# Folding the sequence transform of a Fourier mixing kernel once more for even k: sums and differences of rows s and S/4 - s

## The chip, the cores and the metric

One core of one Trainium2 chip. The metric is the device time of one execution in microseconds, median over runs; executions of one kernel agree within about 0.2% here.

## The reference, cut to what matters

```python
X = np.fft.fft(x, axis=1)            # x: (8, 3008, 256), batch, sequence S, features D
X = np.fft.fft(X, axis=2).real       # only the real part goes on
h = X.reshape(24064, 256) @ w_in     # w_in: (256, 2048)
g = np.maximum(0.01 * h, h)
out = g @ w_out                      # w_out: (2048, 256)
```

## The kernel before

The two products with w_in and w_out take most of the time ("up", line 422, and "down", lines 465 and 485). The feature transform is folded into w_in at the start. The sequence transform remains as matmuls with tables of cosines and sines (lines 350 and 354, tile `dft_ps`). Symmetries shrink it: x is loaded as four mirrored parts that are added and subtracted on VectorE (DVE), output frequencies k are treated by parity c, rows s by parity r. A "unit" is one batch and one parity of k; it has two feature halves (`blk`), so a batch has four transforms.

```python
NI = 3                       # chunks of 128 rows per parity of s: six in all
KW, KF = [377, 376], [189, 188]
...
def fold_rows(t, h):         # mirrored rows and features
    a, z = t[:, h, 0], t[:, h, 1]
    nc.vector.tensor_tensor(a, a, z, op=ALU.add)
    ...
def fold_halves(b, t):       # rows s and S/2 - s
    a, z = t[:, :, 0], t[:, :, 1]
    nc.vector.tensor_tensor(a[:, 0], z[:, 0], z[:, 1], op=ALU.add)
    nc.vector.tensor_tensor(a[:, 1], z[:, 0], z[:, 1], op=ALU.subtract)
    zs[b] = a
...
def sequence(z_of, m, part, c):
    pe, po = dft_ps(), dft_ps()
    kf, kw = KF[c], KW[c]
    tab = tabs[2 * part, c]
    for i, (lo, hi) in enumerate(((0, kf), (kf, 2 * kf), (0, 2 * kf))):     # even s
        nc.tensor.matmul(pe[0:m, lo:hi], lhsT=z_of(i, 0), rhs=tab[:, i * kf : i * kf + hi - lo], ...)
    tab = tabs[2 * part + 1, c].rearrange("p (i k) -> p i k", i=NI)
    for i in range(NI):                                                     # odd s
        nc.tensor.matmul(po[0:m, 0:kw], lhsT=z_of(i, 1), rhs=tab[:, i, 0:kw], ...)
    return pe, po
...
units = [(b, c) for b in range(B) for c in range(2)]                        # even k first
```

One more input, the Nyquist feature of all eight batches, goes through the same transform with 8 stationary columns instead of 128, once per parity. A scheduler decides the order of each engine's queue from the program order, so source order and engine order can differ.

## Time and profile before

| | before |
|---|---|
| median (3 runs) | 1948.77 us (1948.72 to 1948.90) |
| profiled span | 1947.3 us |
| PE busy | 1924.5 us, 99% |
| DVE busy | 1109.9 us, 57% |
| GpSimd (POOL) busy | 1039.1 us, 53% |

The prediction below shows the lines that carry this. In a timeline each line is: start in us, length in us, engine, source line, operation, output and inputs, stationary operand (partitions * columns), moving operand (partitions x columns), how many instructions were merged, and in brackets the idle time before them with what ended it. Each matmul here, of 32-bit data, is recorded twice, each time with a weight load (six records and six loads for the three matmuls at 697.66 us); I call one such pair of load and matmul a record.

### The profile page before, as it was taken

The numbers are of one execution on the slowest core, as the hardware profiler recorded it, in microseconds if no ns is written. First come the engines' busy times: TensorE is split into PE (matmuls) and PEld (weight loads), VectorE is DVE, ScalarE is ACT, GpSimd is POOL, SyncE is SP. The second block draws the span as 40 slices with busy tenths as digits, with TensorE's granted clock in tenths as the row PEclk, the third lists the DMA queues.
The fourth block names the chain that finished last, engine by engine and source line by source line (L and its number), as shares of the span: only waits on it lengthen the run. The fifth ranks groups of instructions, "written<-read, shape, count | busy, mean of one in ns | idle before, by whom it ended". The sixth has DMA issues, their size and how long they took to land.

```text
span 1947.3 us, 24383 instructions
## 1 busy us (share of the span) xinstructions
PE 1924.5 (99%) x8920; PEld 1683.9 (86%) x8920; DVE 1109.9 (57%) x2143; ACT 458.9 (24%) x526; POOL 1039.1 (53%) x1508
## 2 busy tenths in 40 slices
PE   6999999999999999999999999999999999999999
PEld 3788888888888888888888888888888888888888
DVE  8765545575555655466555665547545574555554
ACT  4422222222222222222222222222222222222221
POOL 1115555565555655556555665556645565555554
PEclk9999999999999999999999999999999999999999
DMA  8120000010001000020000200002000020000000
GB/s 300 42 85 20 11 19 22 19 76 11 19 22 76 19 11 30 11 80 15 22 19 12 83 22 12 19 12 83 22 11 19 11 95 12 19 11 22 11 11 22
DMA packets 25598, 70.22 MB, mean 36 GB/s; under 512 B 4596, under 2 KB 17268, under 8 KB 23432
## 3 DMA queue, kind: packets, MB, share of 16 engines
q1 hardware_dynamic: 23360, 68.66, 9.6%
q8 instruction: 71, 1.16, 0.2%
q14 instruction: 47, 0.39, 0.1%
q10 hardware_dynamic: 2120, 0.02, 0.1%
HBM read 43.95 MB, written 24.71 MB: 35 GB/s over the span
## 4 chain that ended last, share of the span: by engine, by line
PE 98%; DVE 1%; DMA 0%; ACT 0%; issue 0%; SPq 0%; DVEq 0%; ACTq 0%
PE sum_ps L485 56%; PE cos_ps L422 17%; PE sin_ps L422 17%; PE dft_ps L354 3%; PE sum_ps L465 3%; PE dft_ps L350 2%; PE up_ps L312 1%; DMA raw<-in_w_in_dram 0%; DVE power L288 0%; DVE wo L289 0%; ACT L433 0%; DVE e L496 0%; DVE wo L287 0%; ACT g L433 0%; SPq L260 0%
## 5 line engine op out<-in xcount | busy, mean ns | idle before, releaser
L427 DVE SCALAR_TENSOR_TENSOR cos<-nb,wn,cos_ps 128x251 f32<-128x251 f32 (+1 forms) x768 | 330.7, 472 | 721.2 <-PE cos_ps L422 721.1
L433 ACT ACTIVATE g<-g 128x1004 f32<-128x1004 f32 (+1 forms) x384 | 399.1, 1039 | 1208.3 <-DVE g L432 1199.9
L440 POOL TENSOR_TENSOR s<-g 128x251 f32<-128x251 f32 (+1 forms) x368 | 271.8, 739 | 761.1 <-ACT g L433 761.1
L485 PE MATMUL sum_ps<-s,wt 128*128 128x251 f32 (+1 forms) x2208 | 527.7, 374 | 0.0
L485 PEld LDWEIGHTS sum_ps<-s,wt 128*128 128x128 f32 x2208 | 415.9, 188 | 52.4
L422 PE MATMUL cos_ps<-mix,wf 128*128 128x251 f32 (+1 forms) x1536 | 387.9, 375 | 0.0
L422 PE MATMUL sin_ps<-mix,wf 128*128 128x251 f32 (+1 forms) x1536 | 387.6, 374 | 0.0
L485 PE MATMUL sum_ps<-g,wo 128*128 128x251 f32 (+1 forms) x1472 | 371.9, 374 | 0.0
L422 PEld LDWEIGHTS cos_ps<-mix,wf 128*128 128x128 f32 x1536 | 291.2, 190 | 35.8 <-issue 1.6
L422 PEld LDWEIGHTS sin_ps<-mix,wf 128*128 128x128 f32 x1536 | 290.3, 189 | 35.2 <-PE up_ps L312 0.2
L485 PEld LDWEIGHTS sum_ps<-g,wo 128*128 128x128 f32 x1472 | 279.4, 190 | 38.7
L431 DVE TENSOR_TENSOR g<-cos,sin_ps 128x502 f32<-128x502 f32 (+1 forms) x384 | 260.1, 677 | 50.0 <-DVE cos L427 8.9
L441 POOL TENSOR_TENSOR s<-s,g 128x251 f32<-128x251 f32 (+1 forms) x368 | 278.8, 758 | 0.0
L443 POOL TENSOR_TENSOR s<-g,s 128x251 f32<-128x251 f32 (+1 forms) x368 | 262.6, 714 | 28.6
L432 DVE TENSOR_TENSOR g<-cos,sin_ps 128x502 f32<-128x502 f32 (+1 forms) x384 | 257.3, 670 | 0.0
L442 POOL TENSOR_TENSOR s<-g 128x251 f32<-128x251 f32 (+1 forms) x368 | 243.2, 661 | 0.0
L485 PE MATMUL sum_ps<-g,wt 128*128 128x251 f32 (+1 forms) x736 | 215.8, 375 | 0.0
L485 PE MATMUL sum_ps<-s,wo 128*128 128x251 f32 (+1 forms) x736 | 215.7, 375 | 0.0
L485 PEld LDWEIGHTS sum_ps<-s,wo 128*128 128x128 f32 x736 | 139.4, 189 | 16.4
L485 PEld LDWEIGHTS sum_ps<-g,wt 128*128 128x128 f32 x736 | 139.8, 190 | 15.8
L496 DVE TENSOR_TENSOR o<-e,sum_ps 128x251 f32<-128x251 f32 (+1 forms) x184 | 67.5, 409 | 8.7 <-ACT e L494 8.7
L354 PE MATMUL dft_ps<-tab,xt 128*128 128x377 f32 (+1 forms) x192 | 66.0, 479 | 0.0
(53 smaller groups left out, 598.1 us busy)
## 6 DMA issues: line engine op xcount, KB each, us to landing
xt<-in_x_dram SPq DMA_DIRECT2D x16, 1536.0 KB, 10.0
out_dram<-o SPq DMA_DIRECT2D x80, 251.0 KB, 2.3
raw<-in_w_in_dram SPq DMA_DIRECT2D x8, 512.0 KB, 5.4
raw<-in_w_out_dram SPq DMA_DIRECT2D x8, 512.0 KB, 3.9
out_dram<-o SPq DMA_DIRECT2D x16, 250.0 KB, 2.3
nb<-nyq_dram SPq DMA_DIRECT2D x8, 376.5 KB, 4.8
nb<-nyq_dram SPq DMA_DIRECT2D x8, 376.0 KB, 3.2
tab<-in_seq_tab_dram SPq DMA_DIRECT2D x4, 565.5 KB, 10.7
```

What stands on the lines that cost most here:

```text
L354: nc.tensor.matmul(po[0:m, 0:kw], lhsT=z_of(i, 1), rhs=tab[:, i, 0:kw], start=(i == 0), stop=(i == NI - 1))
L422: nc.tensor.matmul(pt[blk][:, h * n : (h + 1) * n], lhsT=wf[:, blk, fs], rhs=mixed[b, c][blk][:, at : at + n], start=True, stop=True)
L427: nc.vector.scalar_tensor_tensor(cos[:, hs], in0=spreads[b, c][:, at : at + n], scalar=wn[:, h * NH + f : h * NH + f + 1], in1=pt[0][:, hs ...
L431: nc.vector.tensor_tensor(g[:, 0], cos[:, 0 : 2 * n], pt[1][:, 0 : 2 * n], op=ALU.add)
L432: nc.vector.tensor_tensor(g[:, 1], cos[:, 0 : 2 * n], pt[1][:, 0 : 2 * n], op=ALU.subtract)
L433: nc.scalar.activation(g, g, ACT.Lrelu)
L440: nc.gpsimd.tensor_tensor(s1, a[1][0], a[1][1], op=ALU.add)
L441: nc.gpsimd.tensor_tensor(s2, s1, a[0][0], op=ALU.subtract)
L442: nc.gpsimd.tensor_tensor(s3, a[0][0], a[1][0], op=ALU.subtract)
L443: nc.gpsimd.tensor_tensor(s4, a[0][1], s2, op=ALU.subtract)
L485: nc.tensor.matmul(sums[j][p], lhsT=still[p], rhs=moving[p], start=(f == 0 and i % 2 == 0), stop=(f == NH - 1), skip_group_check=True)
L496: nc.vector.tensor_tensor(to, x, y, op=ALU.add)
```

## The change

For even k the table of row S/4 - s equals that of row s up to a sign that alternates with k/2. So the two rows can be added for half of the frequencies and subtracted for the other half, and each matmul needs half the columns. The outputs go to every second column. To let the rows meet on the same partition, x is laid out in seven chunks instead of six (four of 95 rows for even s, three for odd s), and DVE makes the sums and differences ("quarter folds"). Odd k, which needs no quarter folds, now comes first in each batch. Core of the diff:

```diff
-NI = 3
+NI = [4, 3]
+NT = 7
+PE_ROWS = 95
+PO_ROWS = 60
+PARITIES = (1, 0)
...
+    def fold_quarters(src, sums, last, tmp):
+        for op, to in zip((ALU.add, ALU.subtract), sums):
+            nc.vector.tensor_tensor(to[0:PE_ROWS, 0:2], src[0:PE_ROWS, 0:2], src[0:PE_ROWS, 2:4], op=op)
+            nc.vector.tensor_tensor(to[:, 4], src[:, 4], src[:, 5], op=op)
+        lo, hi = slice(0, PO_ROWS), slice(P // 2, P // 2 + PO_ROWS)
+        nc.scalar.copy(tmp[0][lo], src[hi, 6])
+        nc.scalar.copy(tmp[1][hi], src[lo, 6])
+        nc.vector.tensor_tensor(last[lo], src[lo, 6], tmp[0][lo], op=ALU.add)
+        nc.vector.tensor_tensor(last[hi], tmp[1][hi], src[hi, 6], op=ALU.subtract)
...
-        for i, (lo, hi) in enumerate(((0, kf), (kf, 2 * kf), (0, 2 * kf))):
+        for i in range(n):                                       # even s: n = 4
+            if c == 1:
+                still, to = rows[0:PE_ROWS, i], pe[0:m, i % 2 * kf : (i % 2 + 1) * kf]
+            else:
+                q, p = divmod(i, 2)
+                still, to = rows[0][(p + part) % 2][0:PE_ROWS, q], pe[0:m, q * kf + p : (q + 1) * kf : 2]
...
-        for i in range(NI):
-            nc.tensor.matmul(po[0:m, 0:kw], lhsT=z_of(i, 1), rhs=tab[:, i, 0:kw], start=(i == 0), stop=(i == NI - 1))
+        for i in range(n):                                       # odd s: n = 3
+            if c == 1:
+                still, to = rows[:, NI[0] + i], po[0:m, 0:kw]
+            elif i < 2:
+                still, to = rows[0][(i + part) % 2][:, NI[0]], po[0:m, i:kw:2]
+            else:
+                still, to = rows[1], po[0:m, 0:kw]
...
-    units = [(b, c) for b in range(B) for c in range(2)]
+    units = [(b, c) for b in range(B) for c in PARITIES]
...
+            if n > 0 and n % 2 == 0 and part > 0 and f == 1:
+                fold_x_quarters(b, part - 1)
```

More of the change, by code (lines that the diff above doesn't have):

```diff
@@ L62 @@
 KP = [1, 0]
-TW = [4 * KF[0], NI * KC]
+TW = [[4 * PE_ROWS, 2 * KW[0]], [4 * KF[1], 3 * KW[1]]]
+PARITIES = (1, 0)
 UW = [753, 752]
@@ L78, in m_order @@
     at = np.arange(P)[:, None]
-    if r == 1:
-        m = at + P * np.arange(NI)
-        return np.where(m < 376, m, -1)
+    if r == 0:
+        m = np.concatenate([2 * at, 2 * at + 1, 376 - 2 * at, 375 - 2 * at], axis=1)
+        last = np.array([188, 187, 190, 189])
+        return np.where(at < PE_ROWS - (last != 188), m, -1)
     half = at // (P // 2)
-    m = np.concatenate([2 * at, 2 * at + 1, 2 * (P + at - half * (P // 2)) + half], axis=1)
-    return np.where(m < 377, m, -1)
+    m = P + at % (P // 2)
+    m = np.where(at % (P // 2) < PO_ROWS, np.where(half, 375 - m, m), -1)
+    return np.concatenate([at, 375 - at, m], axis=1)
 def k_order(c):
@@ L93, in laid_out @@
 def laid_out(x):
-    m = np.stack([m_order(0), m_order(1)], axis=-1)
-    rows = 2 * m + np.arange(2)
+    m = np.concatenate([m_order(0), m_order(1)], axis=1)
+    rows = 2 * m + np.repeat([0, 1], NI)
     d = np.concatenate([np.arange(P + 1), np.arange(D - 1, P, -1)])
@@ L111, in seq_tables, with values @@
 def seq_tables():
-    out = np.zeros((4, 2, P, TW[1]), np.float32)
-    for r in range(2):
-        m = m_order(r)
-        s = 2 * m + r
-        weight = np.where(m < 0, 0.0, np.where((s == 0) | (s == Q), 0.5, 1.0))
-        for c in range(2):
-            k = k_order(c)
-            turn = (s[:, :, None] * k) % S
-            turn = np.where(turn > H, turn - S, turn)
-            a = 2.0 * np.pi * turn / S
-            cos = weight[:, :, None] * np.where(4 * np.abs(turn) == S, 0.0, np.cos(a))
-            sin = weight[:, :, None] * np.where(np.abs(turn) == H, 0.0, np.sin(a))
-            for n, t in ((r, cos), (2 + r, sin)):
-                if r == 1:
-                    out[n, c].reshape(P, NI, KC)[:, :, : KW[c]] = t
-                    continue
-                kf = KF[c]
-                t = t[:, :, :kf]
-                parts = [t[:, 0], t[:, 1], t[:, 2] * (m[:, 2:] % 2 == 0), t[:, 2] * (m[:, 2:] % 2 == 1)]
-                out[n, c, :, : 4 * kf] = np.concatenate(parts, axis=1)
+    out = np.zeros((4, 2, P, TW[1][1]), np.float32)
+    def values(m, r, c):
+        s, k = 2 * m + r, k_order(c)
+        weight = np.where(m < 0, 0.0, np.where((s == 0) | (s == Q), 0.5, 1.0))[:, :, None]
+        turn = (s[:, :, None] * k) % S
+        turn = np.where(turn > H, turn - S, turn)
+        a = 2.0 * np.pi * turn / S
+        cos = np.where(4 * np.abs(turn) == S, 0.0, np.cos(a))
+        sin = np.where(np.abs(turn) == H, 0.0, np.sin(a))
+        return weight * cos, weight * sin
+    for r in range(2):
+        for part, t in enumerate(values(m_order(r), r, 1)):
+            if r == 0:
+                t = t[:, :, : KF[1]]
+            out[2 * part + r, 1, :, : TW[1][r]] = t.reshape(P, -1)
+    for part, t in enumerate(values(m_order(0), 0, 0)):
+        for q in range(2):
+            for p in range(2):
+                v = t[:, q, p : KF[0] : 2]
+                at = (2 * q + p) * PE_ROWS
+                out[2 * part, 0, :, at : at + v.shape[1]] = v
+    m = m_order(1)
+    m[P // 2 :, 2] = m[: P // 2, 2]
+    difference = np.arange(P)[:, None] // (P // 2)
+    for part, t in enumerate(values(m, 1, 0)):
+        last = t[:, 2] * ((np.arange(KW[0]) + part) % 2 == difference)
+        out[2 * part + 1, 0, :, : TW[0][1]] = np.concatenate([t[:, 0, 0::2], t[:, 0, 1::2], last], axis=1)
     return out
@@ L155, in chunks @@
     for b in range(B):
-        for c in range(2):
+        for c in PARITIES:
             for j in range(0, UW[c], CW):
@@ L203, in load_x @@
     def load_x(b, q=None):
-        t = xp.tile([P, 2, 2, NI * 2, D], F32, tag="x", bufs=1, name="xt")
+        t = xp.tile([P, 2, 2, NT, D], F32, tag="x", bufs=1, name="xt")
         for h in range(2):
-            (q or nc.sync).dma_start(t[:, h], x[b, :, h].rearrange("p e i r d -> p e (i r) d"))
+            (q or nc.sync).dma_start(t[:, h], x[b, :, h])
         return t
@@ L226, in fold_halves, with fold_x_quarters @@
         nc.vector.tensor_tensor(a[:, 1], z[:, 0], z[:, 1], op=ALU.subtract)
-        zs[b] = a
+        zs[b] = t
+    def fold_quarters(src, sums, last, tmp):
[7 more added lines that the diff above has]
+        nc.vector.tensor_tensor(last[hi], tmp[1][hi], src[hi, 6], op=ALU.subtract)
+    def fold_x_quarters(b, part):
+        src, z = zs[b][:, part, 0, :, part * P : (part + 1) * P], zs[b][:, part, 1]
+        halves = [z[:, :, i * P : (i + 1) * P] for i in range(2)]
+        fold_quarters(src, halves, halves[0][:, 5], [h[:, 6] for h in halves])
+        quarters[b, part] = halves, halves[0][:, 5]
+    quarters = {}
     feat_sb = const.tile([P, 2, 2 * P], F32, name="feat_sb")
@@ L234, in tile_fnet_leaky_relu @@
     wt = const.tile([P, 4, NH, P], F32, name="wt")
-    nyx = const.tile([P, 2, 2, NI, 2, B], F32, name="nyx")
+    nyx = const.tile([P, 2, 2, NT, B], F32, name="nyx")
     inf = const.tile([P, 2], F32, name="inf")
@@ L240, in load_tab @@
     def load_tab(q, n, c):
-        t = const.tile([P, TW[n % 2]], F32, name=f"tab_{n}_{c}")
-        q.dma_start(t, seq_tab[n, c, :, 0 : TW[n % 2]])
+        t = const.tile([P, TW[c][n % 2]], F32, name=f"tab_{n}_{c}")
+        q.dma_start(t, seq_tab[n, c, :, 0 : TW[c][n % 2]])
         tabs[n, c] = t
@@ L340, in combine_w_out, with sequence @@
             nc.gpsimd.tensor_tensor(to, x, y, op=ALU.subtract)
-    def sequence(z_of, m, part, c):
+    def sequence(rows, m, part, c):
         pe, po = dft_ps(), dft_ps()
         kf, kw = KF[c], KW[c]
-        tab = tabs[2 * part, c]
-        for i, (lo, hi) in enumerate(((0, kf), (kf, 2 * kf), (0, 2 * kf))):
-            nc.tensor.matmul(pe[0:m, lo:hi], lhsT=z_of(i, 0), rhs=tab[:, i * kf : i * kf + hi - lo],
-                             start=(i == 0), stop=(i == NI - 1), skip_group_check=True)
-        tab = tabs[2 * part + 1, c].rearrange("p (i k) -> p i k", i=NI)
-        for i in range(NI):
-            nc.tensor.matmul(po[0:m, 0:kw], lhsT=z_of(i, 1), rhs=tab[:, i, 0:kw], start=(i == 0), stop=(i == NI - 1))
+        tab, n = tabs[2 * part, c], NI[0]
+        for i in range(n):
[4 more added lines that the diff above has]
+                still, to = rows[0][(p + part) % 2][0:PE_ROWS, q], pe[0:m, q * kf + p : (q + 1) * kf : 2]
+            at = i * TW[c][0] // n
+            nc.tensor.matmul(to, lhsT=still, rhs=tab[0:PE_ROWS, at : at + to.shape[1]],
+                             start=(i == 0), stop=(i == n - 1), skip_group_check=True)
+        tab, n, at = tabs[2 * part + 1, c], NI[1], 0
+        for i in range(n):
[5 more added lines that the diff above has]
+                still, to = rows[1], po[0:m, 0:kw]
+            nc.tensor.matmul(to, lhsT=still, rhs=tab[:, at : at + to.shape[1]],
+                             start=(i == 0), stop=(i == n - 1), skip_group_check=True)
+            at += to.shape[1]
         return pe, po
@@ L373, in dft @@
         b, c = u
-        z = zs[b]
-        sums = sequence(lambda i, r: z[:, (c + blk) % 2, 2 * i + r, blk * P : (blk + 1) * P], P, blk, c)
+        if c == 1:
+            rows = zs[b][:, 1 - blk, 0, :, blk * P : (blk + 1) * P]
+        else:
+            rows = quarters.pop((b, blk))
+        sums = sequence(rows, P, blk, c)
         def rest():
@@ L392, in nyquist @@
     def nyquist(c):
-        sums = sequence(lambda i, r: nya[:, c, i, r, :], B, 0, c)
+        if c == 1:
+            rows = nya[:, 1]
+        else:
+            halves = [nyb[:, 0], nyb[:, 1]]
+            fold_quarters(nya[:, 0], halves, halves[0][:, 5], [h[:, 6] for h in halves])
+            rows = halves, halves[0][:, 5]
+        sums = sequence(rows, B, 0, c)
         def rest():
@@ L510, in step @@
                 if part == 0:
-                    if c == 1:
+                    if n % 2 == 1:
                         t = xs.pop(b + 1)
@@ L517, in step @@
                     dft(units[n + 1], part - 1)()
-            if c == 0 and part == 2 and f == 6 and b + 1 < B:
+            if n % 2 == 0 and part == 2 and f == 6 and b + 1 < B:
                 xs[b + 1] = load_x(b + 1)
@@ L532, in tile_fnet_leaky_relu @@
     for n in range(4):
-        load_tab(nc.sync, n, 0)
+        load_tab(nc.sync, n, 1)
     convert(w0)
@@ L542, in tile_fnet_leaky_relu @@
     fold_halves(0, t0)
-    nyquist(0)()
+    nyquist(1)()
     dft(units[0], 0)()
@@ L568, in tile_fnet_leaky_relu @@
     for n in range(4):
-        load_tab(nc.sync, n, 1)
+        load_tab(nc.sync, n, 0)
     convert(o)
+    for blk in range(2):
+        fold_x_quarters(0, blk)
     some_steps(plain)
-    nyquist(1)()
+    nyquist(0)()
     spread(units[1])
@@ L590 @@
         "x": x,
-        "x_nyq": x[..., P].transpose(1, 2, 3, 4, 5, 0),
+        "x_nyq": x[..., P].transpose(1, 2, 3, 4, 0),
         "w_in": moe_w_in,
```

## The prediction

> **What bounds the kernel now.** I read the page first: the busy shares, the slices, the chain that ended last.
>
> ```profile
> PE 1924.5 (99%) x8920; PEld 1683.9 (86%) x8920; DVE 1109.9 (57%) x2143; ACT 458.9 (24%) x526; POOL 1039.1 (53%) x1508
> ...
> PE 98%; DVE 1%; DMA 0%; ACT 0%; issue 0%; SPq 0%; DVEq 0%; ACTq 0%
> PE sum_ps L485 56%; PE cos_ps L422 17%; PE sin_ps L422 17%; PE dft_ps L354 3%; PE sum_ps L465 3%; PE dft_ps L350 2%; PE up_ps L312 1%; DMA raw<-in_w_in_dram 0%; DVE power L288 0%; DVE wo L289 0%; ACT L433 0%; DVE e L496 0%; DVE wo L287 0%; ACT g L433 0%; SPq L260 0%
> ```
>
> The reader is to see that the matmul engine is the bound, and that the change touches a small part of it: the two dft_ps lines are 3% + 2% of the span, about 105 us. A busy PE is not yet a saturated one, so I asked for busy time by stretch (columns: length, then busy time and instruction count of each engine, granted clock, DMA share, GB/s).
>
> ```profile
> 0.00:50.00 50.00, 31.66 (x89) 17.50 (x90) 43.11 (x82) 21.62 (x34) 4.91 (x10) 0.93 0.82 293
> 50.00:140.00 90.00, 90.00 (x407) 75.12 (x406) 64.86 (x116) 29.14 (x39) 14.39 (x21) 1.00 0.18 60
> 140.00:500.00 360.00, 360.00 (x1685) 318.12 (x1685) 198.14 (x387) 82.99 (x92) 202.99 (x297) 1.00 0.08 28
> ...
> 1000.00:1500.00 500.00, 500.00 (x2339) 441.28 (x2338) 283.86 (x547) 113.66 (x127) 285.88 (x412) 1.00 0.08 30
> ```
>
> After 50 us PE has no idle time, at full clock. So every array cycle removed there is time removed, as long as nothing else starts to hold PE up. The first 50 us are different: PE works 32 of them, DVE 43. Next the timeline of one transform of 128 features at about 698 us:
>
> ```profile
> 697.66 1.44 PE L350 MATMUL dft_ps<-tab,xt 128*128 128x189 f32 x6
> 698.94 2.07 PE L354 MATMUL dft_ps<-tab,xt 128*128 128x377 f32 x6
> 700.85 0.37 PE L485 MATMUL sum_ps<-g,wo 128*128 128x251 f32 x1
> ```
>
> Starts count, not durations, because matmuls overlap. Each matmul is recorded twice (six records for three matmuls). The even part, four records of 189 columns and two of 378, takes 698.94 - 697.66 = 1.28 us for 1512 columns; the odd part, six of 377, takes 1.91 us for 2262. Both are 0.845 ns per column and record: here the moving columns alone set the time. One such transform costs 3.19 us.
>
> [...]a load of 128 columns lasts 189 ns and one of 8 columns (the Nyquist rows) 90 ns, so 120 columns cost about 99 ns, with some 83 ns fixed. [...]the 189-column records start every 160 ns though each needs a load recorded at 189 ns.[...]
>
> **The change part by part.** (1) Even k, even s: three matmuls (189 + 189 + 378 = 756 columns) become four of 95, 94, 95, 94 (378 columns). By columns that is 2 x 378 x 0.845 = 0.64 us. But eight records now each need a new 128-column weight load, and a load starts only when the previous matmul starts.[...] (2) Even k, odd s: 3 x 377 = 1131 columns become 189 + 188 + 377 = 754: 2 x 754 x 0.845 = 1.27 us instead of 1.91. These are long enough for their loads (160 ns is seen). One even-k transform thus goes from 3.19 to 2.15 us, 1.04 saved; there are 8 batches x 2 feature halves, 16 x 1.04 = 16.6 us. The one Nyquist transform of even k has 8-column loads, so its short records aren't bound by them: 3.19 to 1.91, 1.3 us more. (3) Odd k: 4 x 188 and 3 x 376 columns, as many as before; 17 transforms with one more matmul each, 0.1 us. PE therefore gives up 16.6 + 1.3 - 0.1 = 17.8 us.
>
> (4) DVE and DMA get more: x has seven chunks instead of six, so loads and folds grow by 1/6. The folds were 28.5 + 19.4 + 18.2 + 16.0 + 14.0 = 96 us, so +16 us; the new quarter folds are 16 x (two of 95x256, two of 128x128, two of 60x128), at rates of existing SBUF operations some 0.35 + 0.35 + 0.2 x 4 = 1.5 us, +24 us. DVE goes to about 1150 us of 1930, 60%: hidden on average, and the question is the burst after each x load. (5) The start: odd k comes first, and its first transform needs the difference of the halves, which DVE makes after the sum.
>
> The start, worked along DVE's queue: before, DVE folds x from 16.34 us and the first x transform starts at 25.48, when the half sum is ready. After: row folds 2 x (2.1 + 1.0 + 1.0), small Nyquist folds 0.7, Nyquist butterfly 0.3, both half folds 2 x 1.95 = 13.1 us, so 29.4 us, 4 us later. PE then idles over 5 us before it, long enough to lose the clock, perhaps 2.5 us more. Against that stands the wait that follows:
>
> ```profile
> 34.55 1.01 PE L422 MATMUL sin_ps<-mix,wf 128*128 128x251 f32 x4
> 41.35 3.72 PE L465 MATMUL sum_ps<-g,wo 128*128 128x251 f32 x8 [5.79 <-ACT g L433]
> 44.86 1.86 PE L312 MATMUL up_ps<-win,feat_sb 128*128 128x512 f32 x2
> ```
>
> Here PE waits 5.8 us, and then runs cold (eight records of 251 columns need 3.5 us instead of 1.7). The order of the changed program puts fifteen down matmuls ahead of the next weight fold, so this wait and the cold stretch shrink. Walking both queues with the durations above I lose 1.3 us by the end of that weight fold and about 1 us in the next: +2.5 us, range 0 to 5. Sum: 1948.8 - 17.8 + 2.5 = 1933.5 us.
>
> **Rivals.** First, **the DVE burst becomes a wait of PE**. In the trace before, around the fold at 1340 us (the longest wait for x):
>
> ```profile
> 1339.91 2.19 DVE L215 TENSOR_TENSOR xt<-xt 128x1536 f32<-128x1536 f32 x1 [1.36 <-DMA xt<-in_x_dram]
> ...
> 1355.16 2.09 DVE L226 TENSOR_TENSOR xt<-xt 128x1536 f32<-128x1536 f32 x1
> 1357.17 0.67 DVE L431 TENSOR_TENSOR g<-cos,sin_ps 128x502 f32<-128x502 f32 x1
> 1357.76 0.67 DVE L432 TENSOR_TENSOR g<-cos,sin_ps 128x502 f32<-128x502 f32 x1
> 1358.35 0.85 DVE L427 SCALAR_TENSOR_TENSOR cos<-nb,wn,cos_ps 128x251 f32<-128x251 f32 x2
> ```
>
> The second g of that step normally frees a PSUM pair 6.0 us before PE needs it; here it came 5.9 us late, a margin of 0.12 us. In the other five bursts like it the margins are 1.3 to 1.9 us. With folds a sixth longer, and x landing later (first half 6.3 us after issue; about 4.2 of it transfer, so +0.7), the same order would stall PE. But the changed program's order puts one fold operation between every cos pair and every g pair, where the old one often put two. Walking it from a first fold at 3.2 us after a cos start, with PE's step of 4.66 us: g pairs come late by 1.9, 2.5, 2.6, 4.2, then 1.8 us, and the quarter folds fall behind that. 4.2 is under 6.0, so no stall; with the longest x wait, 5.3. If I am wrong by 2 us in each of seven bursts, the time is 1945. Second, **the weight loads bind harder**: if the whole 190 ns must pass per short record, the even part takes 1.52 us instead of 1.28, an even-k transform saves only 0.4 us, and the time is about 1944. The 160 ns pitch speaks against it. Third, **the loads bind not at all** (82 ns a record): 0.22 us more per transform, 1930. Fourth, a price of stride-2 PSUM writes: nothing speaks for it; doubled time for those records would cost about 1.3 us a transform, and eat the gain.
>
> **Range and chances.** The gain can't exceed about 21.5 us (16 x 1.26 + 1.3), 1.1% of the time, so faster by over 2% (39 us) is out of reach; slower by over 2% would need several new waits at once. Predicted 1933.5 us, range 1928 (loads hidden, or a free start) to 1943 (loads or bursts costing about 9 us): same 0.98, others 0.01 each.
>
> **What would show it.** In the timeline of an even-k transform: start to start of the eight 95- and 94-column records 0.88 us (0.64: loads hidden; 1.5: whole loads count), then 1.27 us for the odd part. PE still without idle time after 60 us, at clock 1.00, and PE's first sum_ps at about 43 to 45 us instead of 41.35. DVE near 1150 us, with no PE wait on DVE's g or on POOL in the bursts. The prediction is wrong if stride-2 writes or weight loads stretch those records, if PE waits a few us after each x load, or if the start loses more than 5 us.

The forecast's sum came to 1948.8 - 17.8 + 2.5 = 1933.5 us. One term of the 17.8 was built on a load time that was taken from no trace: a short record at 110 ns, so 8 x 0.110 = 0.88 us for the even part, which with 1.27 us for the odd part makes the 2.15 us of an even-k transform and the 1.04 us saved. An estimate from the trace before comes close: loads of 128 and of 8 columns last 189 and 90 ns, 99 ns for 120 columns, so 106 ns for 128; and in the transform at 697.66 us each load starts 1 to 2 ns after a matmul starts. Together that is about 108 ns a record, if nothing but that part of the load has to fit, which was an assumption. The clock that a gap costs is seen in the same trace: after the 5.79 us of waiting before 41.35 us the mean granted clock was 0.50 until 44.86 us; after the 1.84 us before 25.48 us it was 1.00 until 28.74 us. That the new gap would cost 2.5 us was a guess. The 4.2 us of transfer for half of x is near the trace: its two halves, 3.15 MB, moved in some 8.7 us (1333.4 to 1342.1 us), 4.3 us each.

## The result, and the profile after

| | before | after |
|---|---|---|
| median | 1948.84 us (6 runs) | 1936.82 us (6 runs, 1935.49 to 1937.37) |
| profiled span | 1947.3 us | 1935.4 us |
| PE busy | 1924.5 us | 1909.9 us |
| DVE busy | 1109.9 us | 1149.3 us |
| mean granted clock | 0.998 | 0.996 |

The ratio of after to before is 0.9937, 95% interval 0.9924 to 0.9949; a ratio is the mean time of one kernel's runs over that of the other's of the same rounds, so not quite the ratio of the medians. The change won 12.0 us where 15.3 were forecast.

The page after, busy shares and chain:

```profile
PE 1909.9 (99%) x8988; PEld 1687.9 (87%) x8988; DVE 1149.3 (59%) x2245; ACT 468.6 (24%) x560; POOL 1055.4 (55%) x1508
...
PE 98%; DMA 1%; DVE 0%; issue 0%; ACT 0%; SPq 0%; ACTq 0%; DVEq 0%
```

PE is still the bound. The same stretches as before (columns as in the prediction: length, busy time and count of PE, weight loads, DVE, ScalarE (ACT) and GpSimd, clock, DMA share, GB/s):

```profile
0.00:50.00 50.00, 28.86 (x81) 17.28 (x82) 39.26 (x75) 18.97 (x33) 3.25 (x10) 0.87 0.73 267
50.00:140.00 90.00, 90.00 (x418) 76.06 (x417) 76.50 (x145) 32.86 (x49) 12.22 (x18) 1.00 0.21 75
140.00:500.00 360.00, 360.00 (x1706) 320.57 (x1705) 207.09 (x408) 85.23 (x98) 208.75 (x300) 1.00 0.08 30
```

After 50 us PE has no idle time, as before. In the first 50 us it works 28.9 us instead of 31.7, at a mean granted clock of 0.87 instead of 0.93. One even-k transform after, to hold against the one at 698 us before:

```profile
579.22 1.03 PE L402 MATMUL dft_ps<-tab,xt 95*128 95x95 f32 x8
580.08 1.47 PE L412 MATMUL dft_ps<-tab,xt 128*128 128x189 f32 x6
581.39 0.37 PE L554 MATMUL sum_ps<-g,wo 128*128 128x251 f32 x1
```

From start to start the eight short records take 0.86 us and the odd part 1.31, together 2.17 instead of 3.19 us. Single records show why it is not 0.64 for the short ones: their weight loads start at 579.223, 579.333, 579.444, 579.556 us, one every 110 to 112 ns, and the matmuls follow at that pace. The Nyquist transform is a control in the same trace. It has the same 95 rows, the same columns and the same stride-2 outputs, but 8 stationary columns:

```profile
83.07 0.83 PE L402 MATMUL dft_ps<-tab,nyx 95*8 95x95 f32 x8
83.73 1.44 PE L412 MATMUL dft_ps<-tab,nyx 128*8 128x189 f32 x6
```

Its eight records take 0.66 us, 83 ns each: that is near the pace of the columns alone (80 ns at 0.845 ns each). The last view after is PE at the start, to hold against the lines from 34.55 us in the prediction:

```profile
22.09 2.06 PE L412 MATMUL dft_ps<-tab,nyx 128*8 128x376 f32 x6
31.48 2.85 PE L402 MATMUL dft_ps<-tab,xt 95*128 95x188 f32 x8 [7.33 <-issue]
34.12 3.54 PE L412 MATMUL dft_ps<-tab,xt 128*128 128x376 f32 x6
37.50 1.44 PE L402 MATMUL dft_ps<-tab,xt 95*128 95x188 f32 x8
...
47.15 8.33 PE L534 MATMUL sum_ps<-g,wo 128*128 128x251 f32 x30 [2.86 <-ACT g L502]
```

The first x transform starts at 31.48 us (before: 25.48) and takes 37.50 - 31.48 = 6.02 us, the second (same shape) 3.17: after the gap of 7.33 us PE ran at about half clock, and again after the second wait, of 2.86 us. The granted clock, 0.53 in both, stands third from the right:

```profile
31.48:37.50 6.02, 6.02 (x15) 4.52 (x15) 3.63 (x10) 4.19 (x9) 0.00 (x0) 0.53 0.53 154
47.15:50.75 3.60, 3.60 (x9) 2.94 (x10) 3.60 (x10) 2.80 (x5) 0.00 (x0) 0.53 0.13 49
```

The first down matmul starts at 47.15 us (before: 41.35), after a shorter wait, 2.86 instead of 5.79 us.

To put one number on the start, I added up PE's lost time up to 100 us: the time to its first matmul, plus for every record its start-to-start time beyond what a record of that width takes in the steady stretch (short records are priced by their columns, 80 ns). Before: 24.6 us. After: 29.9 us. So the start lost 5.2 us in these two traces; with short records priced at the 110 ns that they take it is 5.0, and the trace of an unedited repeat gives 4.6 to 4.8.

### The profile page after: what moved, and what is told of

Same layout as the page of the kernel before. It is cut to its first block, busy times and chain, and to the rows that moved or that the text cites. A ratio compares the mean times of both kernels' runs of the same rounds, so it can differ in the third digit from the quotient of the medians.

```text
span 1935.4 us, 24654 instructions
## 1 busy us (share of the span) xinstructions
PE 1909.9 (99%) x8988; PEld 1687.9 (87%) x8988; DVE 1149.3 (59%) x2245; ACT 468.6 (24%) x560; POOL 1055.4 (55%) x1508
## 3 DMA queue, kind: packets, MB, share of 16 engines
q1 hardware_dynamic: 23360, 72.09, 10.1%
## 4 chain that ended last, share of the span: by engine, by line
PE 98%; DMA 1%; DVE 0%; issue 0%; ACT 0%; SPq 0%; ACTq 0%; DVEq 0%
PE sum_ps L554 56%; PE cos_ps L491 17%; PE sin_ps L491 17%; PE sum_ps L534 3%; PE dft_ps L412 3%; PE dft_ps L402 2%; PE up_ps L357 1%; DMA raw<-in_w_in_dram 0%; DMA wn_dram<-wf 0%; DVE power L333 0%; DVE e L565 0%; DVE cos L496 0%; ACT g L502 0%; ACTq L369 0%; SPq L305 0%
## 5 line engine op out<-in xcount | busy, mean ns | idle before, releaser
L509 POOL TENSOR_TENSOR s<-g 128x251 f32<-128x251 f32 (+1 forms) x368 | 265.5, 721 | 727.1 <-ACT g L502 722.6
L512 POOL TENSOR_TENSOR s<-g,s 128x251 f32<-128x251 f32 (+1 forms) x368 | 273.0, 742 | 28.9
L500 DVE TENSOR_TENSOR g<-cos,sin_ps 128x502 f32<-128x502 f32 (+1 forms) x384 | 259.5, 676 | 47.9 <-DVE cos L496 11.3
L510 POOL TENSOR_TENSOR s<-s,g 128x251 f32<-128x251 f32 (+1 forms) x368 | 271.4, 738 | 0.0
L511 POOL TENSOR_TENSOR s<-g 128x251 f32<-128x251 f32 (+1 forms) x368 | 263.6, 716 | 0.0
L501 DVE TENSOR_TENSOR g<-cos,sin_ps 128x502 f32<-128x502 f32 (+1 forms) x384 | 257.2, 670 | 0.0
L534 PE MATMUL sum_ps<-g,wo 128*128 128x251 f32 x256 | 58.8, 383 | 2.9 <-ACT g L502 2.9
```

The costliest lines, as they stand in the source:

```text
L500: nc.vector.tensor_tensor(g[:, 0], cos[:, 0 : 2 * n], pt[1][:, 0 : 2 * n], op=ALU.add)
L501: nc.vector.tensor_tensor(g[:, 1], cos[:, 0 : 2 * n], pt[1][:, 0 : 2 * n], op=ALU.subtract)
L509: nc.gpsimd.tensor_tensor(s1, a[1][0], a[1][1], op=ALU.add)
L510: nc.gpsimd.tensor_tensor(s2, s1, a[0][0], op=ALU.subtract)
L511: nc.gpsimd.tensor_tensor(s3, a[0][0], a[1][0], op=ALU.subtract)
L512: nc.gpsimd.tensor_tensor(s4, a[0][1], s2, op=ALU.subtract)
```

## The experiments

Medians are of four to six runs each; "before" stood at 1948.3 to 1948.85 us beside them. An unedited run of the changed kernel in the last group of runs gave 1936.83 us (1935.97 to 1937.27), so differences below 0.7 us are not read.

> The changed kernel itself, unedited, on the chip and in the rounds of the two runs beside it, to compare them with. All theories: 1936.8 us within 0.8 us.

### What each of the two folds is worth

**Even-s fold undone**: the four chunks go in unfolded.

```diff
-                still, to = rows[0][(p + part) % 2][0:PE_ROWS, q], pe[0:m, q * kf + p : (q + 1) * kf : 2]
+                still, to = rows[2][0:PE_ROWS, i], pe[0:m, i % 2 * kf : (i % 2 + 1) * kf]
```

(with the table of 4 x 189 columns and without the DVE additions and subtractions of chunks 0 to 3)

> The changed kernel with the even-s fold of even k undone (four matmuls of 189 columns from the unfolded chunks; the odd-s fold stays). Theory (short records last 110 ns, set by the 128-column weight load): the even part of an even-k transform goes from 0.88 to 1.28 us, 16 x 0.39 + 0.63 for the Nyquist one = +6.9 us, so about 1943.7 us, if the start stays as it is (its order may move by 2 us). Rival (the short records gain nothing, because loads or stride-2 writes eat it): 1936.8 us, unchanged.

Measured: 1943.85 us (1943.72 to 1944.57), correct; 7.0 us above the changed kernel, where 6.9 were expected.

**Odd-s fold undone**: three matmuls of 377 columns from the unfolded chunks 4 to 6.

```diff
-            elif i < 2:
-                still, to = rows[0][(i + part) % 2][:, NI[0]], po[0:m, i:kw:2]
-            else:
-                still, to = rows[1], po[0:m, 0:kw]
+            else:
+                still, to = rows[2][:, NI[0] + i], po[0:m, 0:kw]
```

(with the table of 3 x 377 columns and without the DVE and ScalarE operations of the quarter fold on chunks 4 to 6)

> The changed kernel with the odd-s fold of even k undone (three matmuls of 377 columns; the even-s fold stays). Theory: the odd part goes from 1.31 us (traced after) to 1.90 us, 16 x 0.59 + 0.63 = +10.1 us, about 1946.9 us. If the two folds are independent, the sum of both undone differences is the whole gain of PE, about 17 us. Rival (something shared, as DVE bursts or the start, sets the time): both undone versions move by less than half of that.

Measured: 1946.93 us (1946.67 to 1947.84), correct; 10.1 us above, as expected. The two add up to 17.1 us. The whole change won 12.0. The difference, 5.1 us, agrees with what the start loses in the traces (4.6 to 5.2 us). The starts of the two undone versions lose as much as the changed kernel's (29.4 and 29.1 us in the reckoning above), so what they gave up is PE's work and not the start. PE's gain is there in full, and the start gives back 30% of it.

### What sets the 110 ns of a short record

**Unit stride** (wrong result): neighbouring output columns instead of every second one.

```diff
-                ... pe[0:m, q * kf + p : (q + 1) * kf : 2]
+                ... pe[0:m, q * kf + p * 95 : q * kf + p * 94 + 95]
-                ... po[0:m, i:kw:2]
+                ... po[0:m, i * 189 : 189 + i * 188]
```

> Wrong result on purpose: the outputs of the stride-2 matmuls go to neighbouring columns instead of every second one; counts, columns and loads unchanged. Theory (weight load sets the short records): they stay at 110 ns, the time stays at 1936.8 us within 1 us. Rival (stride-2 PSUM writes cost the 28 ns): the records fall to 82 ns, 16 x 8 x 0.028 = 3.6 us less, about 1933.2 us.

Measured: 1936.62 us (1935.80 to 1936.91). One transform of it:

```profile
578.90 1.02 PE L402 MATMUL dft_ps<-tab,xt 95*128 95x95 f32 x8
579.76 1.47 PE L412 MATMUL dft_ps<-tab,xt 128*128 128x189 f32 x6
```

Still 0.86 us for the eight records: the stride does not set the 110 ns. A price of the stride below the 28 ns that the load adds could hide behind it here; but the Nyquist records, with stride 2 and narrow loads, take 83 ns, and the 189-column records start every 160 ns with stride 2 as they did without. So the runs show no price of the stride.

**Half loads**: each short matmul of the x transforms split into two of 64 stationary columns.

```diff
+            cuts = [(0, m // 2), (m // 2, m)] if c == 0 and m == P else [(0, m)]
+            for lo, hi in cuts:
+                nc.tensor.matmul(to[lo:hi], lhsT=still[:, lo:hi], rhs=..., ...)
```

> Each short matmul of an even-k transform is split into two of 64 stationary columns (correct result): 16 records instead of 8, each with a load of half the width. Theory (a record lasts as long as the longer of its columns and the streaming part of the next load):[...] the columns bind at 82 ns, 16 x 0.082 = 1.31 us instead of 0.88, +6.9 us, about 1943.7 us. Rival a (a fixed floor of 110 ns for a record, not the load): 16 x 0.110 = 1.76 us, +14 us, about 1951. Rival b (the two halves run side by side[...]): 0.88 us or less, 1936.8 us or less.

Measured: 1938.78 us (1938.45 to 1939.10), correct. Neither the 1943.7 of my theory nor rival a.

```profile
579.09 0.38 PE L493 MATMUL sin_ps<-mix,wf 128*128 128x251 f32 x1
579.40 0.88 PE L404 MATMUL dft_ps<-tab,xt 95*64 95x95 f32 x16
580.21 1.54 PE L414 MATMUL dft_ps<-tab,xt 128*128 128x189 f32 x6
581.59 0.37 PE L556 MATMUL sum_ps<-g,wo 128*128 128x251 f32 x1
```

The two halves run side by side (rival b): the single records start in pairs 7 ns apart, and the pairs follow each other at about 82 ns (the second after 133), the pace of 95 columns. Sixteen records take 0.81 us from the first start to the next width's start, and most of the tail of that is a wait. The loads are narrower (133 to 138 ns recorded instead of 190) and no longer bind. What eats this gain is the passage between widths: the full record before the first half record lasts 0.31 us instead of 0.21, the last pair is followed by the next record only after 0.18 us, and the first 189-column record then takes 0.26 us, against 0.19 in the changed kernel. From 579.09 to 581.59 us this is 2.50 us; the same stretch of the changed kernel, one 251-column record (0.21) and its transform (2.17), is 2.38. Sixteen times 0.12 is 1.9 us, the measured 2.0. So the width of the load explains 110 ns, the stride does not, and splitting loads is not worth its passages here. (A narrower load also means fewer output rows of the matmul; no run separates the two.)

### What the start loses, and why

Four versions each change one thing at the start. In this table, in us, each row but for the last column is from one profiled run: PE's first matmul (it moves by up to 1 us from run to run with the first weights' arrival), start of the first x transform, its length, start of the first down matmul, lost time up to 100 us as defined above (extra matmuls counted as lost), median time. The unedited repeat loses 29.5 us in the same reckoning where the changed kernel's first trace has 29.9, so differences of half a us in that column are not read.

| version | first matmul | first x transform | its length | first down | lost | time |
|---|---|---|---|---|---|---|
| before | 10.72 | 25.48 | 3.26 | 41.35 | 24.6 | 1948.8 |
| changed | 10.95 | 31.48 | 6.02 | 47.15 | 29.9 | 1936.8 |
| wn on SyncE | 10.20 | 28.81 | 5.69 | 45.68 | 29.3 | 1936.7 |
| difference first | 10.43 | 28.40 | 5.93 | 45.94 | 29.4 | 1937.4 |
| extra matmuls | 11.17 | 31.15 | 3.24 | 46.61 | 27.6 | 1935.1 |
| even k first | 10.17 | 30.16 | mixed | 44.76 | 31.3 | 1939.0 |
| three edits | 10.20 | 27.30 | 3.79 | 42.91 | 25.9 | 1933.5 |
| three + GpSimd | 10.51 | 27.19 | 3.79 | 44.63 | 27.2 | 1933.6 |

**wn on SyncE.** My walk had the first x transform at 29.4 us; it came 2 us later. DVE and ScalarE of the changed kernel at that time:

```profile
24.26 1.08 DVE L242 TENSOR_TENSOR xt<-xt 128x889 f32<-128x889 f32 x1
27.17 0.34 DVE L424 TENSOR_TENSOR ev<-e,dft_ps 8x188 f32<-8x188 f32 x1 [1.83 <-ACT e L423]
27.44 2.00 DVE L249 TENSOR_TENSOR xt<-xt 128x1792 f32<-128x1792 f32 x1
29.37 2.01 DVE L250 TENSOR_TENSOR xt<-xt 128x1792 f32<-128x1792 f32 x1
```

```profile
25.82 0.97 ACTq L369 DMA_DIRECT2D wn<-wn_dram  x2
26.83 0.30 ACT L423 COPY e<-dft_ps 8x188 f32<-8x188 f32 x1 [3.37 <-issue]
```

DVE waits 1.83 us for a small copy of ScalarE before it makes the half sums (L249, L250). ScalarE's copy (26.83 us) stands in its queue behind the issue of a DMA (wn, 25.82 us), which waits for another DMA to land (wn_dram, issued at 21.54 us and landed 4.27 us later, at 25.81). In the kernel before, the copy (22.38 us) stood ahead of that issue (25.98 us).

```diff
-                nc.scalar.dma_start(wn[:, h * NH + at : ...
+                nc.sync.dma_start(wn[:, h * NH + at : ...
```

> The changed kernel with the two small reloads of wn issued from the SyncE queue instead of ScalarE's. Theory (in the changed order ScalarE stands in its queue on the landing of wn_dram before it can copy e for the Nyquist rows, and DVE waits 1.8 us for that copy before the half folds): the first x transform starts at about 29.7 instead of 31.5 us, ScalarE has no wait there, and the time falls by about 1.8 us to 1935.0. Rival (that wait is beside the path, the end of the start is set by DVE's later work or by the weight loads, which now stand behind wn in SyncE's queue): no change or slower, 1936.8 us or more.

Measured: 1936.69 us (1936.32 to 1937.96). The wait is gone and the first transform starts 1.9 us sooner after PE's first matmul, but the first down matmul hardly does (0.7 us), and the time does not move. The theory fell in this form: this wait is not what the time hangs on alone. (The move also puts wn into the queue of the weight loads; whether a gain was lost there was not tested.)

**Difference first.**

```diff
-        nc.vector.tensor_tensor(a[:, 0], z[:, 0], z[:, 1], op=ALU.add)
-        nc.vector.tensor_tensor(a[:, 1], z[:, 0], z[:, 1], op=ALU.subtract)
+        nc.vector.tensor_tensor(a[:, 1], z[:, 0], z[:, 1], op=ALU.subtract)
+        nc.vector.tensor_tensor(a[:, 0], z[:, 0], z[:, 1], op=ALU.add)
```

> The changed kernel with the difference of the halves made before the sum, as odd k (which now comes first) needs it. Theory: the first x transform starts one half fold (1.95 us) earlier, at about 29.5 us, and the time falls by up to 2 us, to about 1934.9. Rival (DVE's work up to the first g sets the start, not when PE begins): the first transform starts earlier, the first down matmul at 47 us does not, 1936.8 us.

Measured: 1937.37 us (1936.59 to 1938.39). Again the transform starts earlier and nothing comes of it, as the rival said. In both versions PE still has a gap of over 5 us before the first transform, runs that transform at about half speed (5.69 and 5.93 us, where the second takes 3.17), and then waits longer for the first g (4.4 and 4.8 us instead of 2.9).

**Extra matmuls.**

```diff
     nyquist(1)()
+    pt = up_ps("warm_ps")
+    for i in range(10):
+        nc.tensor.matmul(pt[0:B, 0:KW[1]], lhsT=nya[:, 1, NI[0]], rhs=tabs[1, 1][:, 0:KW[1]], start=..., stop=...)
     dft(units[0], 0)()
```

> The changed kernel with ten extra matmuls (8 stationary columns, 376 moving, result unused) in the idle time before the first x transform, about 6.3 us of PE work at full clock. Theory (the 7.5 us gap drops PE to half clock and the first transform of 3.2 us takes 6.0): the clock stays at 1.0, the first transform takes 3.2 us, and most of that is won: about 1934 us. Rival (PE's slow transform is hidden behind DVE's work): the first down matmul comes at 47 us as before, 1936.8 us.

Measured: 1935.06 us (1934.77 to 1935.69), 1.8 us less. The first transforms:

```profile
23.78 6.48 PE L474 MATMUL warm_ps<-tab,nyx 128*8 128x376 f32 x20
31.15 1.51 PE L402 MATMUL dft_ps<-tab,xt 95*128 95x188 f32 x8 [0.89 <-issue]
32.50 2.06 PE L412 MATMUL dft_ps<-tab,xt 128*128 128x376 f32 x6
34.39 1.44 PE L402 MATMUL dft_ps<-tab,xt 95*128 95x188 f32 x8
```

The clock holds through it: the transform takes 3.24 us, instead of 6.02 at a granted clock of 0.53. Half speed comes later: from 43.28 to 46.61 us eight records of 251 columns take 3.33 us, against some 1.7 in the steady stretch. Of the 2.8 us won there 1.8 arrive in the time; the rest turns into waits for DVE's `mix` (3.2 us before one group). The scheduler also ordered the queues differently in this version, so not all of the 1.8 us need be the clock.

**Even k first again.**

```diff
-PARITIES = (1, 0)
+PARITIES = (0, 1)
```

(with the calls at the start swapped, and the quarter folds made right after the half folds)

> The changed kernel with even k first again (the folds and tables as changed; the quarter folds then stand before the first transform). Theory (the start is limited by DVE's queue, and 3 us of quarter folds replace the 1.8 us wait and a later sum): about even, 1936 to 1938 us. Rival (odd k first is what cost the start 5 us): 1933 us or less. If bursts with urgent quarter folds hold PE up, stretches after 150 us lose a few us each, and the time goes over 1940.

Measured: 1938.99 us (1938.45 to 1940.09), 2.2 us slower than odd k first, 1 us more than I expected. So the order odd k first is not what costs the start; it saves some of it.

**The three edits together**, with six extra matmuls, for the gap is shorter now:

> The changed kernel with the three start edits together: wn reloads from SyncE, difference first, and six extra matmuls that keep the clock up until the first x transform. Theory (the start is set by DVE's queue from 16 us on; each edit alone moved PE's first transform but only what takes waits out of DVE's queue counts): the extra matmuls' 1.7 us plus the last DVE wait of 1.3 us, about 1934 us, below the warm one alone (1935.1) by 1 us. Rival (edits that start PE earlier add up: 1.7 + 2 + 2): 1931 us.

Measured: 1933.48 us (1932.99 to 1934.63), correct: 3.35 us less than the unedited run beside it, and their ranges do not meet. This is 1.6 us less than extra matmuls alone, so the two edits that did nothing alone seem to count once the clock holds; this is argued from two versions that also differ in the number of extra matmuls and ran in different groups. DVE's only wait between 15 and 50 us is 0.64 us, and lost time is 25.9 us, 1.3 more than in the kernel before. It is the fastest version found, 0.9924 of before.

**Three edits, and the first batch's half sum on GpSimd.**

```diff
-        nc.vector.tensor_tensor(a[:, 0], z[:, 0], z[:, 1], op=ALU.add)
+        (nc.gpsimd if b == 0 else nc.vector).tensor_tensor(a[:, 0], z[:, 0], z[:, 1], op=ALU.add)
```

> As the run beside it, and for the first batch the half sum (one operation of 128x1792, 1.95 us of DVE at the start) goes to GpSimd, which is idle then. Theory (DVE's queue sets the start): 1.95 us less work ahead of the first g, about 1.5 to 2 us below the run beside it, about 1932 us, and PE's first down matmul that much earlier. Rival (PE or the weight loads set the start by now): no change; or slower, if GpSimd's sum (about 5 us at its rate of some 2.9 ns per element) arrives too late for the second x transform.

Measured: 1933.57 us (1931.20 to 1934.59), no difference to the run beside it that this spread would show; the profiled run is the slowest of the four. DVE and GpSimd in this run:

```profile
27.92 0.53 DVE L428 TENSOR_TENSOR nyq<-ev,dft_ps 8x376 f32<-8x376 f32 x1
28.37 2.84 DVE L319 TENSOR_SCALAR wo<-raw 128x512 int32<-128x512 int32 x1
31.14 0.41 DVE L320 TENSOR_SCALAR power<-raw 128x512 int32<-128x512 int32 x1
```

```profile
25.08 5.85 POOL L250 TENSOR_TENSOR xt<-xt 128x1792 f32<-128x1792 f32 x1 [2.12 <-DVE xt L242]
```

GpSimd's addition takes 5.85 us, to 30.9 us (the 2.9 ns per element of the expectation is the pace of its additions of 128x251 in the trace before, 649 to 766 ns on average by line; here it is 3.3). Meanwhile a DVE operation (L319) that takes 0.41 us in the run beside it takes 2.84, and ends 0.28 us after GpSimd's addition. The 1.95 us of work left DVE, and this one operation took 2.4 us longer. Others beside the same addition did not (L249 took 2.01 us, L427 and L428 0.53 each; in the changed kernel 2.00 and 0.53), and no view tells why L319 did. So the run does not test what it was for: whether DVE's amount of work alone sets the start stays open.

## Why the prediction was right, point by point

- **PE's gain in the even part.** It put a short record at about 110 ns and the part at 0.88 us; measured 110 to 112 ns and 0.86 us. Stride, as rival four had it, is excluded by the unit-stride run. Rival two (whole loads, 1.5 us) and rival three (no binding, 0.64 us) are excluded by the trace; the Nyquist records (83 ns with 8-column loads) and the half-load run (82 ns with 64-column loads) point to the load's width.
- **Odd part.** 1.27 us predicted, 1.31 measured: the record after the first of 189 columns starts 191 ns after it instead of 160, and its load starts 33 ns after a matmul's start (580.083, 580.116 us), as among the short records (28 to 33 ns), instead of 1 to 3 ns.
- **Sum for PE.** 17.8 us predicted; 17.1 us by the two undone folds.
- **DVE.** 1150 us predicted, 1149.3 measured, and this is luck in part. By instruction times the folds of rows and halves grew from 96.1 to 105.6 us, +9.5 where 16 were forecast, and the quarter folds take 42.6 us where 24 were forecast (an operation of 95x256 takes 0.58 us on average, not 0.35). Busy time grew by only 39.4 us because instruction times overlap (at 637.36 us L500 lasts 660 ns, and L501 starts after 586).
- **Bursts.** The first rival did not come about. PE has no wait from 100 us to the tail. DVE waits 0.6 to 0.9 us for x in six bursts, and its g comes late by at most 3.1 us of 6.0, where I had walked to 4.2. The smallest margin after such a burst is 2.9 us (2.2 in the unedited repeat); before it was 0.12. The 1945 us that the prediction gives for this rival does not follow from its own numbers: seven stalls of 2 us would be 1947.5. That the finer interleaving of the folds does this is read from the two traces and their orders, and no run undid it alone.
- **The start: the term that was mis-sized.** "+2.5 us, range 0 to 5": it measured 4.6 to 5.2 us, at the 5 us that the prediction itself named as a sign of being wrong, and this is most of the 3.3 us by which the forecast time missed; the rest is the 0.7 us by which PE's gain fell short. The walk along DVE's queue took for granted that nothing stands in it. I had not walked ScalarE's queue, where a DMA issue stood ahead of the copy; that wait is 1.83 us of the delay, and the first transform comes at 31.5 instead of 29.4 us. The half clock cost 2.85 us where I had guessed 2.5. My first down matmul at 43 to 45 us came at 47.15. I had counted on the later wait and the cold stretch to give back 4 us (4 + 2.5 - 2.5): the wait shrank by 2.9 us, the weight folds lost 0.5 us less, and the cold down matmuls lost 2.0 us in both kernels. So they gave back some 3.5 us, while the first transform came 6.0 us later.
- The runs do not pin the 5.2 us on one cause. Any one edit that starts PE earlier is given back, in the later wait and at half clock; the extra matmuls, which hold the clock, are worth 1.8 us, the three edits together 3.35 us. What is left, about 1.3 us of lost time against before, may be the larger folds (1/6 more rows): by the traced durations they stand some 1.5 us longer in DVE's queue before the first transform. This was not tested.

## What to carry to other kernels

When matmuls get narrow, look at the pace of their weight loads too: here a record of 95 moving columns took 110 ns with 128 stationary columns, 83 ns with 8, and pairs with 64 each followed at 82. Price such a record by what the trace shows for its load's width, not by its columns alone. A gain on a saturated engine need not arrive in full when the start changes (here 12.0 of 17.1 us): walk every queue that feeds the first matmul, those with small copies and DMA issues too, and count the clock that a gap costs (here 6.02 instead of 3.17 us for the first transform, after a gap of 7.33 us). When several causes overlap at a start, undoing one at a time can show nothing for each; undo them together before you call any of them harmless.
